# Dense GELU forward and backward on one core: x's first block without overlap, w1 in four parts, the first pair's halves side by side

## The chip, the cores and the metric

The kernel runs on one core of a Trainium2 chip. The time is device microseconds (us) of one execution, as the median of several runs; lower is better. A profiled execution gives the trace from which the views below come.

## The reference

`x` is [2048, 448], `w1` [448, 1792], `w2` [1792, 448], all bf16. Computed are the forward output and the gradients of all five inputs for a given `grad_out`:

```python
h = gelu_tanh(x @ w1 + b1)
out = h @ w2 + b2
# and, by jax.vjp with grad_out: grads of x, w1, b1, w2, b2
```

## The kernel before

The 2048 rows of x are four blocks of 512 columns once turned (xT), and the 1792 hidden units are 14 tiles of 128, taken two at a time: 28 pairs, pair p in block p // 7. All work is laid down in four lists, one for each engine, that set the order of its instructions: PE_ORDER for TensorE (PE), ACT_ORDER for ScalarE (ACT), DVE_ORDER for VectorE (DVE) and SP_ORDER for the queue that issues most DMAs. An engine runs its list from left to right and waits where an item's inputs or its place are not ready; nothing overtakes.

The names in the lists, with a pair's number p:

- On PE, `W` are wake matmuls of constants and `X` the transposes of x's first block. `u` is x times w1 for a pair (`h` is the same for one half of pair 0's columns), `q` is grad_out times w2 turned, `p` and `o` are h times w2 (the output), and `x1.` and so on are the gradient of x. `B` spreads b2 over all partitions.
- `c` copies a pair's `u` out of its two banks and adds b1 (A is the first tile, B the second; on ACT or DVE). `s` (square), `g` (GELU) and `t` (tanh) are ACT's, `e r y z m n` are DVE's; together they make h and the derivative's factors. `G` multiplies them with `q`, which stands in the banks qb.
- `vo` and `vx` copy output and x's gradient from their banks, `So` and `Sx` store them, `H` and `T` store h and turn the gradient of h.
- Loads: `xr` followed by two tile numbers is rows of x, `L` a part of w1's first 384 rows, `R` w1's last rows, `K` a part of w2, `X` and `Y` on SP are x and grad_out turned by the DMA, `J` and `I` are w2 and w1 turned, `E` small ends.

448 is three and a half tiles of 128. So `u` and `q` are done as matmuls of half height, 64 rows, in slots of two side by side: one in the upper half of the array for one tile of the pair, one in the lower half for the other (`uq_run`). A pair has a run `.1` and a run `.2`, between which the halves change banks; before a run that writes banks which the other half wrote last, PE waits for a word from POOL that the earlier run has ended (`run`). For this the fourth tile of xT holds the last 64 columns of x in its upper half and in its lower half the first 64 once more, shifted by one row, which the overlapping load of 512 columns gives (each row of 448 and 64 of the next). w1's fourth tile holds its last 64 rows (R0, R1) and its first 64 (R2, R3).

The first pair is an exception: its two halves of 256 columns, h0.0 and h1.0, are done by `full_run` with 16 matmuls, 12 over 128 rows and 4 over 64. After x's transposes come, in order, B, the first pair, u1 to u3 and then p0.0, the first output piece. `u` uses banks 4 and 5, but pairs 1 and 2 use 0 and 1, 2 and 3 (`U_BANK`); p's items use 0 to 3.

The u copies stand in buffers ub that pairs share by the table `UB`. When all 28 pairs are done, PE runs the two gradients of w1 (L755) and w2 (L809).

Of the kernel before, what the change touches and what calls it, by code (L numbers as in the profile page):

```python
# [96 lines left out]
x0.1.0.6.1 q9.1 u16.1 q9.2 u16.2 x0.0.0.6.2 q10.1 u17.1 q10.2 u17.2 x0.1.0.6.2 q11.1 x0.0.6.10.1 u18.1 q11.2 u18.2
x0.1.6.10.1 x0.0.6.10.2 x0.1.6.10.2 u19.1 q12.1 u19.2 q12.2 x0.0.10.14.1 u20.1 x0.1.10.14.1 u20.2 x0.0.10.14.2
x0.1.10.14.2 q13.1 o2.0.0.6.1 q13.2 o2.1.0.6.1 o2.0.0.6.2 o2.1.0.6.2 q14.1 o2.0.6.10.1 q14.2 o2.1.6.10.1 o2.0.6.10.2
q15.1 u21.1 q15.2 u21.2 o2.1.6.10.2 o2.0.10.14.1 o2.1.10.14.1 u22.1 q16.1 u22.2 q16.2 o2.0.10.14.2 u23.1 o2.1.10.14.2  # L100
u23.2 q17.1 x1.0.0.6.1 x1.1.0.6.1 q17.2 x1.0.0.6.2 x1.1.0.6.2 x1.0.6.10.1 x1.1.6.10.1 q18.1 x1.0.6.10.2 u24.1 q18.2
u24.2 x1.1.6.10.2 x1.0.10.14.1 x1.1.10.14.1 q19.1 x1.0.10.14.2 q19.2 u25.1 x1.1.10.14.2 u25.2 q20.1 x2.0.0.6.1 q20.2
x2.1.0.6.1 u26.1 x2.0.0.6.2 u26.2 x2.1.0.6.2 q21.1 x2.0.6.10.1 u27.1 q21.2 u27.2 x2.1.6.10.1 x2.0.6.10.2 x2.1.6.10.2
q22.1 x2.0.10.14.1 q22.2 x2.1.10.14.1 x2.0.10.14.2 x2.1.10.14.2 q23.1 o3.0.0.6.1 q23.2 o3.1.0.6.1 o3.0.0.6.2
o3.1.0.6.2 q24.1 o3.0.6.10.1 q24.2 o3.1.6.10.1 o3.0.6.10.2 o3.1.6.10.2 q25.1 o3.0.10.14.1 q25.2 o3.1.10.14.1
o3.0.10.14.2 q26.1 o3.1.10.14.2 q26.2 x3.0.0.6.1 x3.1.0.6.1 q27.1 x3.0.0.6.2 q27.2 x3.1.0.6.2 x3.0.6.10.1 x3.1.6.10.1
# [52 lines left out]
def make_plan(tc, ctx, x, w1, b1, w2, b2, grad_out, out_0, out_1, out_2, out_3, out_4, out_5):  # L159
# [113 lines left out]
    def full_run(w, t, banks, pair, c0, c1):  # L275

        two = []
        for i in (0, 1):
            ft = 2 * (pair % NPB) + i
            for k in range(4):  # L280
                rows = slice(0, 128) if k < 3 else slice(0, 64)
                two.append((k == 3, i, k, lambda i=i, k=k, ft=ft, rows=rows: nc.tensor.matmul(  # L282
                    bk_(banks[i])[:, 0:c1 - c0], lhsT=w[rows, k, ft * P:(ft + 1) * P], rhs=t[rows, k, EDGE + c0:EDGE + c1],
                    start=(k == 0), stop=(k == 3), skip_group_check=True)))
        for _, _, _, product in sorted(two, key=lambda m: m[:3]):
            product()

# [24 lines left out]
    def U(p, d, hf=None):  # L312
# [7 lines left out]
        rd = [part_w1(p), ("w1r", int(p % NPB > 3))] + [("xT", b, h) for h in hs]  # L320
# [3 lines left out]
        if d == 2:  # L324
            rd += [("xe", b), ("w1f", int(p % NPB > 3))]
# [73 lines left out]
    def C(p, h, eng, hf=None):  # L399
# [8 lines left out]
        if eng == "ACT":  # L408
            fn = lambda: nc.scalar.activation(out=out, in_=src, func=ACT.Identity, bias=bias)  # L409
        else:  # L410
            fn = lambda: nc.vector.tensor_scalar(out=out, in0=src, scalar1=bias, scalar2=None, op0=ALU.add)  # L411
# [441 lines left out]
```

## Time and profile before

| | |
|---|---|
| median of 3 runs | 266.15 us (266.08 to 266.22) |
| profiled execution | 265.99 us, span 264.2 us |
| TensorE clock granted | 1.00 |
| PE busy | 260.4 us (99%) |
| DVE busy | 198.9 us (75%) |
| ACT busy | 130.6 us (49%) |
| DMA | 46.10 MB, mean 175 GB/s |

The profiled execution lies 0.16 us under the median, and 1.8 us of it are outside the span. Busy time is a share of the whole span; the first 13 us, in which loads, transposes and the first pairs follow on one another, have other limits than the rest. PEld is PE's loading of weights, which runs beside its matmuls. L238 in a row is the line in `run` through which nearly all matmuls of half height go.

### The profile page before, as it was taken

What the parts mean: (1) busy time and instruction counts of PE and PEld (TensorE: products, weight loads), DVE (VectorE), ACT (ScalarE), POOL (GpSimd) and SP (SyncE); (2) the same over time, 40 slices, a digit from 0 to 9 for tenths busy, and PEclk for the clock granted to TensorE, in tenths of its full rate; (3) what the DMA queues carried; (4) which work ended last, traced back from release to release, by engine and by line L of the source; (5) the groups of instructions that cost most, each with busy time, mean ns of one, the idle gap of its engine ahead of it and who ended that gap; (6) DMA issues with size and microseconds to landing.
All of it is one profiled execution on the core that took longest, in us unless ns stands there. A gap on an engine that the chain in (4) does not pass through costs nothing.

```text
span 264.2 us, 5339 instructions
## 1 busy us (share of the span) xinstructions
PE 260.4 (99%) x2170; PEld 182.7 (69%) x2170; DVE 198.9 (75%) x289; ACT 130.6 (49%) x168; POOL 14.1 (5%) x8
## 2 busy tenths in 40 slices
PE   8999999999999999999999999999999999999995
PEld 4488988888888886677777777765555555555554
DVE  6887998999998789897876998339999999311000
ACT  4899786996998936736696511011112111000001
POOL 0000000000000000000000000000000393400000
PEclk9999999999999999999999999999999999999999
DMA  7999689999999953393665934794799988984221
GB/s 199 278 189 257 118 174 189 333 243 257 229 219 197 231 139 66 87 223 85 74 173 160 291 99 104 132 309 108 164 228 158 168 218 171 244 157 130 69 72 35
DMA packets 120235, 46.10 MB, mean 175 GB/s; under 512 B 96671, under 2 KB 120081, under 8 KB 120210
## 3 DMA queue, kind: packets, MB, share of 16 engines
q1 hardware_dynamic: 119636, 45.43, 76.6%
q8 instruction: 17, 0.28, 0.4%
q10 hardware_dynamic: 574, 0.33, 0.4%
q14 instruction: 8, 0.07, 0.1%
HBM read 7.70 MB, written 14.28 MB: 83 GB/s over the span
## 4 chain that ended last, share of the span: by engine, by line
PE 97%; ACT 1%; DVE 1%; issue 0%; ACTq 0%; DVEq 0%
PE bank L238 46%; PE bank L755 16%; PE bank L809 16%; PE qb L238 16%; PE qb L365 1%; ACT TR L427 1%; PE bank L282 1%; PE bank L564 1%; DVE ub L411 0%; ACT ub L409 0%; DVE TR L432 0%; DVE TR L437 0%; PE qb L630 0%; ACT w_sb L814 0%; ACTq L427 0%
## 5 line engine op out<-in xcount | busy, mean ns | idle before, releaser
L238 PEld LDWEIGHTS <-HG 64*128 64x128 bf16 x896 | 70.9, 94 | 17.8 <-issue 0.7
L238 PE MATMUL qb<-gT,w2Tf 64*128 64x512 bf16 x392 | 55.9, 376 | 0.0
L238 PE MATMUL bank<-xT,w1f 64*128 64x512 bf16 x378 | 53.4, 376 | 0.0
L238 PE MATMUL bank<-w_sb,HG 64*128 64x448 bf16 x448 | 51.2, 349 | 0.4 <-ACT ub L409 0.4
L238 PE MATMUL bank<-w1T_sb,HG 64*128 64x448 bf16 x448 | 48.4, 349 | 0.0
L809 PE MATMUL bank<-w2Tf,HG 128*128 128x448 bf16 (+2 forms) x240 | 42.6, 340 | 0.0
L755 PE MATMUL bank<-w1f,gh_nat 128*128 128x448 bf16 x224 | 42.5, 352 | 0.0
L467 DVE SCALAR_TENSOR_TENSOR HG<-TR,qb 128x1024 bf16<-128x1024 bf16 x28 | 34.1, 1217 | 9.6 <-PE qb L238 9.4
L238 PEld LDWEIGHTS <-w2Tf 64*128 64x128 bf16 x392 | 32.6, 94 | 8.2 <-issue 0.2
L238 PEld LDWEIGHTS <-w1f 64*128 64x128 bf16 x378 | 31.4, 94 | 8.3 <-issue 0.3
L809 PEld LDWEIGHTS <-HG 128*128 128x128 bf16 x240 | 22.9, 98 | 19.8
L755 PEld LDWEIGHTS <-gh_nat 128*128 128x128 bf16 x224 | 21.8, 98 | 20.6 <-issue 0.4
L452 ACT ACTIVATE TR<-TR 128x1024 bf16<-128x1024 bf16 x28 | 29.3, 1050 | 11.3 <-DVE TR L442 11.3
L778 DVE TENSOR_TENSOR w1T_sb<-w1T_sb,gh_nat 128x1792 f32<-128x1792 f32 x14 | 28.4, 2025 | 0.5
L457 DVE TENSOR_SCALAR TR<-TR 128x2048 bf16<-128x2048 bf16 x28 | 19.3, 689 | 8.3 <-ACT TR L452 8.3
L760 ACT ACTIVATE TR<-bank 128x448 bf16<-128x448 f32 x14 | 7.6, 543 | 34.9 <-PE bank L755 34.9
L815 DVE CAST w_sb<-bank 128x448 bf16<-128x448 f32 x6 | 3.7, 624 | 25.9 <-PE bank L809 25.9
L814 ACT CAST w_sb<-bank 128x448 bf16<-128x448 f32 (+2 forms) x9 | 4.4, 490 | 37.7 <-PE bank L809 37.7
L784 POOL PARTITION_ALL_REDUCE w1T_sb<-w1T_sb x1 | 10.7, 10662 | 208.3 <-DVE w1T_sb L782 208.3
L409 ACT ACTIVATE ub<-bank,b1T 128x512 bf16<-128x512 f32 (+1 forms) x26 | 16.2, 666 | 10.9 <-DVE TR L442 6.0
L462 DVE TENSOR_TENSOR TR<-TR 128x1024 bf16<-128x1024 bf16 x28 | 19.2, 686 | 0.2
L447 DVE TENSOR_TENSOR TR<-TR,HG 128x1024 bf16<-128x1024 bf16 x28 | 19.2, 684 | 0.0
(45 smaller groups left out, 183.6 us busy)
## 6 DMA issues: line engine op xcount, KB each, us to landing
hT_dram<-HG SPq DMA_DIRECT2D x28, 256.0 KB, 3.4
out_dram<-st SPq DMA_DIRECT2D x16, 224.0 KB, 2.7
w1f<-in_x_dram SPq DMA_DIRECT2D x2, 896.0 KB
w2Tf<-in_grad_out_dram SPq DMA_DIRECT2D x2, 560.0 KB
out_dram<-w_sb SPq DMA_DIRECT2D x2, 448.0 KB, 2.7
out_dram<-xT SPq DMA_DIRECT2D x2, 384.0 KB, 3.1
w_sb<-in_w_dram SPq DMA_DIRECT2D x1, 672.0 KB
w2Tf<-in_grad_out_dram SPq DMA_DIRECT2D x1, 672.0 KB, 4.6
```

What stands on the lines that cost most here:

```text
L238: m = nc.tensor.matmul(bk_(b)[:, 0:n], lhsT=l, rhs=r, start=st, stop=sp, skip_group_check=True)
L409: fn = lambda: nc.scalar.activation(out=out, in_=src, func=ACT.Identity, bias=bias)
L447: pl.op("DVE", f"R{p}", lambda: nc.vector.tensor_tensor(out=t[:, 1], in0=t[:, 1], in1=hblk(p), op=ALU.mult), [("r", p), ("h", p)], [val((" ...
L452: pl.op("ACT", f"t{p}", lambda: nc.scalar.activation(out=t[:, 0], in_=t[:, 0], func=ACT.Tanh), [("y", p)], [val(("t", p), ("TR0", p % NTR) ...
L457: pl.op("DVE", f"m{p}", lambda: nc.vector.tensor_scalar(out=t[:], in0=t[:], scalar1=1.0, scalar2=None, op0=ALU.subtract), [("t", p), ("r2" ...
L462: pl.op("DVE", f"n{p}", lambda: nc.vector.tensor_tensor(out=t[:, 0], in0=t[:, 0], in1=t[:, 1], op=ALU.mult), [("m0", p), ("m1", p)], [val( ...
L467: pl.op("DVE", f"G{p}", lambda: nc.vector.scalar_tensor_tensor(out=ghblk(p), in0=t[:, 0], scalar=2.0, in1=qb[:, :, :], op0=ALU.subtract, o ...
L755: nc.tensor.matmul(bk_(bk)[:, 0:D], lhsT=gh_nat[:, st // 4, ft, st % 4, :], rhs=x_nat[:, st, :], start=(st == 0), stop=(st == NS - 1))
L760: fn = (lambda dst=dst, src=src: nc.scalar.mul(out=dst, in_=src, mul=-0.5)) if eng == "ACT" else \
L778: nc.vector.tensor_tensor(out=hs3, in0=a, in1=gh_nat[:, st // 4, :, st % 4, :], op=ALU.add)
L784: pl.op("POOL", "gb1", lambda: nc.gpsimd.partition_all_reduce(gb1_w, hsum, channels=P, reduce_op=bass_isa.ReduceOp.add), ["hsc"], ["gb1"], ...
L809: nc.tensor.matmul(bk_(bk)[:, 0:d1 - d0], lhsT=h_nat[ft][:, st, :], rhs=g_nat[:, st, d0:d1], start=(st == 0), stop=(st == NS - 1))
```

## The change

Loads. x's first block is read as it is, 448 columns a row, and the fourth tile of xT gets x's last 128 columns (320 to 447). For it a new tile w1z holds w1's last 128 rows; it lies in a stretch of gh_nat that is not yet used then, and comes in three parts (Z0, Z1 on ACT, Z2 on SP). L now has four parts of 256, 512, 512 and 512 columns in place of five. R and F are the last and the first 64 rows of w1 in one load each, first needed by block 1. b1 and b2 are issued by SP, tiles 0 and 1 of x change queues, and K3 is ahead of K2.

Products. In block 0 `u` goes through `plain`: run .1 has four slots and run .2 three, both from unshifted rows, and the edge copy Dx0 is gone. The first pair does the same in its two halves (h0.1, h0.2, h1.1, h1.2); `full_run` is gone. B runs over 64 rows, of which all but one are zero, and stands between h0.1 and h0.2. Pair 3 uses the banks of qb, and u4.1 stands ahead of p0.0.

The four lists are new throughout: W6 for W7, q0.1 behind more p's, output pieces split at 5 and 10 tiles in place of 6 and 10, many B copies on DVE, 14 ub buffers in place of 10 for the first half.

```diff
-W7 X0 X1 X2 X3 B h0.0 h1.0 u1.1 u2.1 u1.2 u3.1 u2.2 u3.2 p0.0 p0.1 u4.1 p0.2 p0.3 u4.2 p1.0 p1.1 p1.2 u5.1 p1.3 p2.0
+W6 X0 X1 X2 X3 h0.1 B h0.2 h1.1 u1.1 h1.2 u1.2 u2.1 u3.1 u2.2 u3.2 u4.1 p0.0 u4.2 p0.1 p0.2 p0.3 u5.1 p1.0 u5.2 p1.1
...
-xr01 L0 b1 b2 table X1 X3 c0A0 c0A1 s0 g0 c1A s1 c2A c3A s2 g1 g2 c4A g3 g4 t0 c5A t1 g5 s3 s4 c6A t2 g6 c7A s5 g7 t3
+xr12 L0 Z0 Z1 table X1 X3 c0A0 c0A1 s0 g0 s1 c2B c3A s2 c4A g1 g2 g3 c5A g4 g5 t0 c6A t1 g6 s3 s4 c7A t2 g7 c8A s5 g8
...
-ident X0 X2 Dx0 b1T c0B0 c0B1 b2c e0 r0 c1B z0 y0 c2B c3B e1 r1 y1 e2 z1 r2 c4B z2 y2 Dg0 c5B m0 n0 m1 n1 c6B G0 m2 e3 n2
+ident X0 b1T X2 b2c c0B0 c0B1 c1A c1B e0 r0 y0 c2A z0 e1 c3B c4B r1 e2 y1 r2 z1 c5B z2 y2 c6B m0 n0 m1 n1 c7B m2 Dg0
+n2 c8B G0 e3 r3 c9B z3 y3 G1 vo0.2 m3 vo0.3 vo0.0 vo0.1 n3 G2 e4 c11B r4 e5 z4 r5 y4 z5 G3 m4 e6 n4 r6 y5 z6 y6 c13B
...
-xr12 xr24 R0 L1 R2 L2 L3 R1 K0 L4 K1 R3 K2 Y0 X1 J0 K3 J1 J2 E J3 I0 I1 Y1 X2 So0.1 H0 H1 H2 H3 H4 H5 H6 H7 H8 T0 T1
+xr01 xr24 b1 b2 L1 L2 Z2 K0 K1 F L3 R K3 K2 X1 J0 Y0 J1 I0 J2 Y1 E J3 I1 So0.1 X2 So0.0 H0 H1 H2 H3 H4 H5 H6 H7 H8 H9
...
-U_BANK = {1: 0, 2: 2}
+U_BANK = {1: 0, 2: 2, 3: 6}
+ACT_FIRST = (3,)
...
+    w1z = gh_nat[:, 1, :, :, :].rearrange("p f s c -> p (f s c)")[:, 0:F]
...
+        def plain(i, k, low, st, sp):
+            rows = slice(0, 64) if low else slice(64, 128)
+            cols = slice(ft[i] * P, (ft[i] + 1) * P)
+            return (banks[i], c1 - c0, w[rows, k, cols] if k < 3 else w1z[rows, cols], t[rows, k, EDGE + c0:EDGE + c1], st, sp)
+
+        if w is w1_sb and pair < NPB:
+            if d == 1:
+                run([(plain(1, k, True, k == 0, False), plain(0, k, False, k == 0, False)) for k in (0, 1, 2, 3)])
+            else:
+                run([(plain(0, k, True, False, k == 2), plain(1, (0, 1, 3)[k], False, False, k == 2)) for k in (0, 1, 2)])
+            return
...
-    W1_PART = (0, 1, 2, 3, 4, 4, 4)
-    W1_COLS = ((0, 256), (256, 512), (512, 768), (768, 1024), (1024, 1792))
+    W1_PART = (0, 1, 1, 2, 2, 3, 3)
+    W1_COLS = ((0, 256), (256, 768), (768, 1280), (1280, F))
+    REST = (0, 1, 1, 2, 2, 2, 2)
+    REST_COLS = ((0, 256), (256, 768), (768, F))
...
-        if d == 0:
-            pe(f"u{p}.{d}{tag}", lambda: full_run(w1_sb, xT[b % 2], bk, p, *c), rd, vs, ("s256", 8), (None, 0))
-            return
...
-        src = bass.AP(tensor=x2.tensor, offset=x2.offset + t0 * P * D, ap=[[D, P], [P * D, t1 - t0], [1, 4 * P]])
+        src = x2[t0 * P:t1 * P, :].rearrange("(t p) d -> p t d", p=P)
...
+                c = min(k * P, D - P)
-                nc.tensor.matmul(bk_(t)[:, k * P:(k + 1) * P], lhsT=x_rows[:, t, k * P:(k + 1) * P], rhs=ident,
+                nc.tensor.matmul(bk_(t)[:, k * P:(k + 1) * P], lhsT=x_rows[:, t, c:c + P], rhs=ident,
...
-            pe("b2u", lambda: nc.tensor.matmul(bk_(6)[:, 0:D], lhsT=one[0:1, 0:P], rhs=stage[NST - 1][0:1, 0, :], start=True, stop=True,
+            pe("b2u", lambda: nc.tensor.matmul(bk_(6)[:, 0:D], lhsT=one[0:64, 0:P], rhs=stage[NST - 1][0:64, 0, :], start=True, stop=True,
```

How the instructions stand on PE in the first pair. Before, in the middle of h0.0 and at the start of h1.0 (xT0 is x's first block turned, w1f holds w1; bank4 and bank5 are the first half's banks, bank2 and bank3 the second's):

```order
L282 MATMUL bank5_94<-xT0_68,w1f_64 128x256
L282 LDWEIGHTS w1f_64 [waits DMAHW5_49]
L282 MATMUL bank4_93<-xT0_68,w1f_64 128x256
L282 LDWEIGHTS w1f_64
L282 MATMUL bank5_94<-xT0_68,w1f_64 128x256
L282 LDWEIGHTS w1f_64 [waits DVE_49]
L282 MATMUL bank2_91<-xT0_68,w1f_64 128x256 [waits Activation_49]
```

Now, at the end of h0.1, B and the start of h0.2 (gh_nat holds w1z, st2 holds b2):

```order
L240 LDWEIGHTS gh_nat_74 [waits DMAHW4_49]
L240 MATMUL bank5_94<-xT0_68,gh_nat_74 128x256
L240 LDWEIGHTS gh_nat_74
L240 MATMUL bank4_93<-xT0_68,gh_nat_74 128x256
L651 LDWEIGHTS const-bfloat16-1.0
L651 MATMUL qb_88<-st2_83,const-bfloat16-1.0 128x448 [waits DMAHW7_49]
L240 LDWEIGHTS w1f_64 [waits Pool_sequencer_49]
L240 MATMUL bank4_93<-xT0_68,w1f_64 128x256
```

The w1 tail now comes from w1z and waits for Z0, B has moved from ahead of the pair into it, and the run behind B waits for POOL.

How they stand on ACT from the first pair's copies to the copy of u4. Before (TR and HG are the targets of s and g, ub and gh_nat of the copies):

```order
L409 ACTIVATE ub0_75<-bank2_91,b1T_86 128x256 [waits PE_49]
L427 ACTIVATE TR0_78<-ub0_75 128x1024 [waits DVE_49,Activation_49]
L422 ACTIVATE HG_73<-ub0_75 128x1024
L409 ACTIVATE ub1_76<-bank0_89,b1T_86 128x512 [waits PE_49]
L427 ACTIVATE TR1_79<-ub1_76 128x1024 [waits DVE_49,Activation_49]
L409 ACTIVATE ub2_77<-bank2_91,b1T_86 128x512 [waits PE_49]
L409 ACTIVATE gh_nat_74<-bank4_93,b1T_86 128x512 [waits PE_49]
L427 ACTIVATE TR2_80<-ub2_77 128x1024 [waits DMAHW3_49,DVE_49,Activation_49]
```

And now:

```order
L410 ACTIVATE ub0_75<-bank2_91,b1T_86 128x256 [waits DVE_49,PE_49]
L435 ACTIVATE TR0_78<-ub0_75 128x1024 [waits DVE_49,Activation_49]
L430 ACTIVATE HG_73<-ub0_75 128x1024
L435 ACTIVATE TR1_79<-ub1_76 128x1024 [waits DVE_49]
L410 ACTIVATE ub2_77<-bank3_92,b1T_86 128x512 [waits PE_49]
L410 ACTIVATE gh_nat_74<-qb_88,b1T_86 128x512 [waits PE_49]
L435 ACTIVATE TR2_80<-ub2_77 128x1024 [waits DMAHW3_49,DVE_49,Activation_49]
L410 ACTIVATE gh_nat_74<-bank4_93,b1T_86 128x512 [waits PE_49]
```

c1A has left ACT for DVE, c2B stands in place of c2A, pair 3 is copied from qb, and c4A has moved ahead of g1 and g2.

How SP's first loads stand. Before (TR2 takes x's rows, w2_sb w2):

```order
L507 DMA TR2_80<-in_x_dram 128x512
L507 DMA TR2_80<-in_x_dram 128x2x512
L507 DMA w1f_64<-in_w1_dram 64x1024
L507 DMA w1f_64<-in_w1_dram 128x3x256
L507 DMA w1f_64<-in_w1_dram 64x1024 [waits DMAHW0_49]
L507 DMA w1f_64<-in_w1_dram 128x3x256 [waits DMAHW1_49]
```

And now:

```order
L516 DMA TR2_80<-in_x_dram 128x448
L516 DMA TR2_80<-in_x_dram 128x2x448
L516 DMA b1n_85<-in_b1_dram 14x128 [waits Pool_49]
L516 DMA st2_83<-in_b2_dram 1x448 [waits Pool_49]
L516 DMA w1f_64<-in_w1_dram 128x3x512 [waits DMAHW0_49]
L516 DMA w1f_64<-in_w1_dram 128x3x512 [waits DMAHW1_49]
L516 DMA gh_nat_74<-in_w1_dram 128x1024 [waits DMAHW2_49]
```

There are eight DMA semaphores, used in turn; the ninth load and each behind it waits until the load that had its semaphore has landed. L1 was the second load of w1 on SP and waited for nothing; now b1 and b2 are ahead of it, and it waits for xr12.

More of the change, by code (lines that the diff above doesn't have):

```diff
@@ L97 @@
[L97 to L106, printed above, removed]
@@ L273, in unit_run @@
         run(slots)
[L275 to L286, printed above, removed]
     def gap(bank):
@@ L319, in U @@
             vs = [bank(("u", p, 0, hf), bk[0]), bank(("u", p, 1, hf), bk[1])]
[L320 to L325 removed]
+        rd = [part_w1(p)] + [("xT", b, h) for h in hs] + ([("w1z", REST[p])] if b == 0 else ["w1r"])
+        if d == 2 and b > 0:
+            rd += [("xe", b), "w1f"]
         pe(f"u{p}.{d}{tag}", lambda: uq_run(w1_sb, xT[b % 2], bk, p, d, *c), rd, vs,
@@ L411, in C, with after @@
             fn = lambda: nc.vector.tensor_scalar(out=out, in0=src, scalar1=bias, scalar2=None, op0=ALU.add)
-        pl.op(eng, f"c{p}{'AB'[h]}{'' if hf is None else hf}", fn, [uv, "b1T"], [v], ("copy", 512 if hf is None else 256))
+        o = pl.op(eng, f"c{p}{'AB'[h]}{'' if hf is None else hf}", fn, [uv, "b1T"], [v], ("copy", 512 if hf is None else 256))
+        if hf is None and u_banks(p)[0] == 6 and f"c{p}B" in DVE_ORDER.split() and f"c{p}A" in ACT_ORDER.split():
+            if eng == ("DVE" if p in ACT_FIRST else "ACT"):
+                after(o, [("u", p, 1 - h)])
+    def after(o, vs):
+        o["after"] = vs
+        return o
     def hblk(p):
@@ L712, in make_plan @@
         elif t == "Nx":
-            rows_nat("xn", x_nat, x2, [("w1", i) for i in range(len(W1_COLS))] + [("w1r", 0), ("w1r", 1), ("w1f", 0), ("w1f", 1)])
+            rows_nat("xn", x_nat, x2, [("w1", i) for i in range(len(W1_COLS))] + ["w1r", "w1f"])
         elif t == "Ng":
```

97 lines of the change are left out of this document (56 added, 41 removed).

## The prediction

> **What bounds the kernel now.** I read the page first: the engines' busy shares and the chain that ended last.
>
> ```profile
> PE 260.4 (99%) x2170; PEld 182.7 (69%) x2170; DVE 198.9 (75%) x289; ACT 130.6 (49%) x168; POOL 14.1 (5%) x8
> PE 97%; ACT 1%; DVE 1%; issue 0%; ACTq 0%; DVEq 0%
> ```
>
> TensorE (PE) is busy 99% of the span and makes up 97% of the chain, so a change pays only where it removes PE slots or stretches in which PE waits. Then the chain in order of time, for those stretches.
>
> ```profile
> 8.58 1.06 ACT TR L427
> 10.56 0.67 DVE ub L411
> 11.31 1.06 ACT TR L427
> 12.99 10.13 PE bank L238 x98
> 23.77 0.76 PE bank L238 x8
> 24.52 0.86 PE qb L238 x8
> ...
> 176.64 42.48 PE bank L755 x224
> 219.12 42.43 PE bank L809 x240
> ```
>
> Between 8.58 and 12.99 the chain leaves PE for ACT and DVE; behind that it is PE alone. Two matmuls of half height make a slot, so 8 are four slots: 0.86 / 4 = 0.216 us at 512 columns, 0.76 / 4 = 0.189 us at 448. From u1.1 to 176.64 the list holds 385 slots of the first kind (27 u and 28 q of 7) and 448 of the second: 83.3 + 84.7 = 167.95 us. PE's own timeline shows where this stretch begins.
>
> ```profile
> 3.27 0.63 PE L365 MATMUL qb<-const-bfloat16-1.0 128*128 128x512 bf16 x1
> ...
> 5.37 0.36 PE L630 MATMUL qb<-st,const-bfloat16-1.0 1*128 1x448 bf16 x1
> 5.66 2.12 PE L282 MATMUL bank<-xT,w1f 128*128 128x256 bf16 x15
> 7.51 0.39 PE L238 MATMUL bank<-xT,w1f 64*128 64x512 bf16 x1
> ...
> 12.99 1.05 PE L238 MATMUL bank<-w_sb,HG 64*128 64x448 bf16 x8 [0.39 <-ACT ub L409]
> ```
>
> u1.1 starts at 7.51, and 7.51 + 167.95 = 175.46 against 176.64: 1.18 us are lost. The 21 slots from u1.1 to p0.0 would end at 12.05, and p0.0 starts at 12.99, so 0.94 of the 1.18 lie there and only 0.24 in the 163 us behind. (The 0.39 in brackets is smaller because the modelled ends cover the rest.) A gap shows in the weight loads, too:
>
> ```profile
> 8.54 3.57 PEld L238 LDWEIGHTS <-w1f 64*128 64x128 bf16 x35 [0.28 <-issue]
> ```
>
> The first gap, at 8.54, is u2.1 waiting for banks 2 and 3, which the first pair's second half held. In the second, ahead of 12.99, p0.0 waits for the same banks until ACT has copied u2. ACT's and DVE's timelines tell why that is late.
>
> ```profile
> 7.82 0.47 ACT L409 ACTIVATE ub<-bank,b1T 128x256 bf16<-128x256 f32 x1 [0.26 <-PE bank L282]
> ...
> 9.54 1.04 ACT L422 ACTIVATE HG<-ub 128x1024 bf16<-128x1024 bf16 x1
> 10.49 0.67 ACT L409 ACTIVATE ub<-bank,b1T 128x512 bf16<-128x512 f32 x1
> 11.31 1.06 ACT L427 ACTIVATE TR<-ub 128x1024 bf16<-128x1024 bf16 x1 [0.15 <-DVE ub L411]
> 12.28 0.67 ACT L409 ACTIVATE ub<-bank,b1T 128x512 bf16<-128x512 f32 x1
> 12.85 0.68 ACT L409 ACTIVATE gh_nat<-bank,b1T 128x512 bf16<-128x512 f32 x1
> ```
>
> The copy at 12.28 is c2A, queued behind c1A and s1. Back to back, ACT starts the next instruction 0.95 us after one of 1024 columns and 0.57 after a copy.
>
> **The first pair, side by side.** Before, from 5.37 to 7.51: B, then 16 matmuls of 256 columns, with a change between full and half height at each regrouping; 2.14 us. Now 28 half matmuls in 14 slots of 256 / 512 x 0.216 = 0.108, without such changes: 1.52 us, of which h1.2 (0.33) stands behind u1.1. h0.1 needs the copy of X1, done at 5.39 before and, with x's rows an eighth shorter, an estimated 0.1 us earlier. So h0.1 starts at 5.36 and ends at 5.80, B at 5.99. h0.2 swaps the halves' banks right behind B, so it waits for POOL's word that h0.1 has ended; no run before stands that close. Bounds: 0, since B may cover it, and 0.2, the longest such wait among PE's weight loads.
>
> ```profile
> PEld L238 <- POOLq L233: 0.3, 2, 0.2
> ```
>
> I take 0.1: h0.2 ends at 6.42. h1.1 needs the copy of X2, now behind b1T on DVE: 4.28 + 0.69 (X0) + 0.85 (b1T) + 0.69 = 6.5, by these rows:
>
> ```profile
> 4.37 0.69 DVE L571 CAST xT<-bank 128x512 bf16<-128x512 f32 x1 [0.78 <-PE bank L564]
> ...
> 6.13 0.85 DVE L648 STREAM_TRANSPOSE b1T<-b1n 32x32 bf16<-32x32 bf16 x4
> ```
>
> So h1.1 runs from 6.53 to 6.97, u1.1 starts there, 0.54 earlier, and owes 0.33 for h1.2: 0.21 gained. The edge copy (Dx0, one column on DVE) goes at no price, since DVE had idle time there; POOL's one more memset lies in the 2 us before x arrives.
>
> **Loads.** SP issues L1 only when the landing of xr12 has freed a DMA semaphore; before, the load in that place (R2) waited for x in the same way and went out at 3.69:
>
> ```profile
> 1.17 0.42 SPq L507 DMA_DIRECT2D TR<-in_x_dram  x1
> ...
> 3.69 0.48 SPq L507 DMA_DIRECT2D w1f<-in_w_dram  x1
> ...
> 9.30 5.68 SPq L519 DMA_TRANSPOSE gT<-in_grad_out_dram  x1
> ```
>
> So L1 goes out near 3.6. It is twice as large as before (393 KB), and u1.1 and u2.1 both need it. The rates at which loads moved, and how long some took:
>
> ```profile
> 2.00:4.50 2.50, 2.50 (x13) 1.21 (x11) 1.50 (x9) 1.49 (x2) 0.00 (x0) 1.00 1.00 318
> 4.50:7.00 2.50, 2.50 (x23) 1.62 (x21) 2.21 (x7) 1.17 (x2) 0.00 (x0) 1.00 1.03 235
> ```
>
> ```profile
> TR<-in_x_dram SPq DMA_DIRECT2D x1, 256.0 KB, 3.4
> w1f<-in_w_dram SPq DMA_DIRECT2D x1, 576.0 KB, 6.3
> gT<-in_grad_out_dram SPq DMA_TRANSPOSE x1, 9.2
> ```
>
> Ahead of L1 are 857 KB (x 459, L0 197, Z0 66, Z1 131, the biases 4): 795 KB by 4.5 at 318 GB/s, the rest by 4.75. L1 then takes 1.24 us at the rate of x's 1024-byte runs (318), or 1.67 at that of the 512-byte runs that followed (235). Its own runs are 1024 bytes, so I take 1.24. To that comes the time from the last byte to the landing, estimated from xr24: issued at 1.17, it landed 3.4 later, at 4.57, while the 0.72 MB up to its end were moved near 4.1. With 0.5, L1 lands at 6.5, inside 6.97. From the x and w1f rows, by size between 262 KB (3.4) and 590 KB (6.3), 393 KB would take 4.6 us and land at 8.2: a wait of 1.2 us as upper bound. The later parts of w1 and w2 land in the order of their use. The first transposed load, Y0, was issued at 9.30 and landed 9.2 later, at 18.5; now X1 is the first, with 0.85 MB more in front of it (w1z and K3, less x's overlap), 2.7 to 3.6 us at the two rates: 21.2 to 22.1. u7.1, the first to read it, stands at 22.4 by the slots.
>
> **The gap at p0.0.** u1.1, h1.2 and u1.2 run to 8.82. A copy starts some 0.2 behind its last slot, so c0A1 and c0B1 (0.47) end at 8.85, and u2.1, which needs their banks, waits 0.08. c1A and c1B are both DVE's (9.0 to 10.4), s1 runs straight behind g0 at 10.8, c2B at 11.75 to 12.45, c2A on DVE to 12.45. u4.1 uses banks 4 and 5, free since h0, because u3 has moved to the qb banks; with it in front, p0.0 comes up at 8.90 + 18 slots = 12.80 and finds everything ready. The 0.94 shrinks to 0.08. Late next is c5A: behind c4A (14.03, when u4.2 has ended) stand g1, g2, g3, so it ends at 14.03 + 0.57 + 3 x 0.95 + 0.67 = 18.12, and u6.1, due at 17.99, waits 0.18.
>
> **DVE.** It takes the B copies of pairs 8, 9, 11, 13, 14 and others from ACT, some 0.67 us each (the chain's 10.56 row). It had little room from 40 to 60, 19.02 of 20 us busy:
>
> ```profile
> 40.00:60.00 20.00, 20.00 (x200) 17.90 (x197) 19.02 (x32) 17.60 (x22) 0.00 (x0) 1.00 1.08 258
> ```
>
> ```profile
> 37.80 2.22 DVE L487 TENSOR_TENSOR st<-bank,b_bc 128x448 bf16<-128x448 f32 x4
> 39.93 1.21 DVE L467 SCALAR_TENSOR_TENSOR HG<-TR,qb 128x1024 bf16<-128x1024 bf16 x1
> 41.06 0.69 DVE L442 TENSOR_TENSOR TR<-TR,gh_nat 128x1024 bf16<-128x1024 bf16 x1
> 41.66 0.68 DVE L462 TENSOR_TENSOR TR<-TR 128x1024 bf16<-128x1024 bf16 x1
> ```
>
> Steps here are 1.13 for G, 0.55 for vo, 0.60 for the rest. The new list starts q0 some 6 us later, which gives room; the tightest place is q3.1, due at 40.3, which needs G2. G1 starts at 34.3 when q1.2 has ended; then 1.13 + 4 x 0.55 + 2 x 0.60 = 4.53, so G2 runs 38.85 to 40.06: 0.2 to spare. I cost DVE at nothing; with that cover gone, each 0.1 of DVE costs PE 0.1.
>
> **Sum.** 6.97 + 0.33 + 167.95 + 0.08 + 0.18 + 0.24 (as before) = 175.75 in place of 176.64, 0.9 us earlier; the last two stages keep their lists. The profiled execution took 265.99 (span 264.20), so 265.1; the median of the runs shown is 0.16 higher, and the forecast **265.3 us**. About 0.2% (0.53 us) is what a measurement here can tell from no change.
>
> **Rivals.**
>
> *The clock stays at half longer (slower).* W6 is one wake matmul less: the seventh started at 3.27, so the sixth ends there, and x's transposes cannot start before 3.6, a gap of 0.35 us that W7 just filled.
>
> ```profile
> L564 PEld LDWEIGHTS <-TR x14: 104/151/152, 3.7 to 5.0; 128*128 128x128 bf16 x14
> L564 PEld LDWEIGHTS <-TR x3: 98/108/151, 5.0 to 5.2; 128*128 128x128 bf16 x3
> ```
>
> PE came up to speed at about 5.1 us (weight loads 151 ns before, 98 after), 4.3 us after the first wake matmul. If the gap costs it the same stretch of some 3 us again, the 3.1 us from h0.1 to about 8.5, less 0.2 of waits, run at half speed: 1.45 us lost, 266.75 in all, and from 1.43 lost the kernel is slower by over 0.2%. It decides whether x's second transposes still run at 151 ns behind 5.2; for: nothing in this trace starts PE with a hole; against: the hole is a tenth of the stretch. The Trainium skill, "TensorE: Matmul & The Clock Gate", section "Part 1: The HAM clock gate", says the full clock comes after one busy window of about 3.4 us in a free-running count. By that rule the window that closed at 5.1 holds the gap, and the next closes at 8.5; how much idleness it forgives the page does not say. 0.09.
>
> *L1 is late (slower).* Price one for one behind 6.97. The gain is gone at 7.9, and from 8.4 the kernel is slower by over 0.2%, with L1 at 8.7 267.0. For: the upper bound of 8.2; against: the 576 KB row had K0 in front of it. 0.08.
>
> *The wait moves to DVE and ACT.* The margins of 0.2 at q3.1 and of -0.18 at u6.1 are as small as the rows are rough; DVE's 1.0 us of idle time between 40 and 60 stands against four more copies between 28 and 60 (2.7). If PE waits 0.7 more, 266.0: no change. 0.20.
>
> *x's second block is late.* Y0 took 5.7 us to issue in a full queue, and X1 meets a fuller one; with X1 at 24 u7.1 waits 1.6, 266.9. It decides at 22.4; for: the margin is only 0.3 at the slower rate; against: larger runs moved faster. 0.06.
>
> **How the numbers follow.** The forecast has 0.57: nearly all of it faster. Rival by rival, DVE/ACT gives 0.03 faster, 0.14 same, 0.03 slower; clock 0.02 and 0.07, L1 0.03 and 0.05, X1 0.01 and 0.05 (same and slower); 0.02 of the forecast falls within. Faster 0.58, same 0.22, slower 0.20. With every wait at zero (0.08 + 0.18 + 0.1) the time is 264.9; a little under that and the rivals up to 266.9 make the range, 264.8 to 266.9.
>
> **What would show it.** Right: h0.1 near 5.4, u1.1 near 7.0, no gap at p0.0, q0.1 near 28.4, the last L238 slot ending near 175.8. Wrong: weight loads of 151 ns behind 5.2; a DMA wait at u1.1 or u7.1; DVE busy without a hole while PE waits at a q; a last slot at or behind 176.6.

## The result and the profile after

| | before | after |
|---|---|---|
| median | 266.15 us (265.94 to 266.81, 20 runs) | 265.74 us (265.52 to 266.22, 20 runs) |
| profiled execution, span | 265.99, 264.2 | 265.63, 263.9 |
| ratio, 95% interval | | 0.9983 (0.9976 to 0.9990) |

By the medians the change makes the kernel 0.41 us (0.15%) faster, about half of the 0.85 forecast.

The page after, busy times and then the chain by engine:

```profile
PE 259.9 (98%) x2181; PEld 187.4 (71%) x2181; DVE 205.4 (78%) x300; ACT 124.1 (47%) x156; POOL 14.5 (5%) x9
PE 97%; DVE 1%; issue 0%; ACT 0%
```

PE still carries the chain. ACT has left it (it was 1%); DVE's 1% now lies ahead of the first transpose. The chain in order of time, at the last two stages:

```profile
176.31 42.48 PE bank L775 x224
218.79 42.43 PE bank L829 x240
```

Both stages start 0.33 earlier than before (176.64 and 219.12) and last as long: all of the gain arises ahead of them. In before's timeline the first transpose stands here, for comparison:

```profile
3.74 1.70 PE L564 MATMUL bank<-st,TR 128*128 128x128 bf16 x16
```

The timeline of after, from the start to p0.0:

```profile
0.86 0.47 POOL L665 MEMSET st<- 64x448 bf16 x1
0.89 1.22 DVE L561 TENSOR_SCALAR st<-st 128x1 bf16<-128x1 bf16 x5
...
3.41 0.93 SPq L516 DMA_DIRECT2D w1f<-in_w_dram  x2
...
3.99 1.80 PE L574 MATMUL bank<-st,TR 128*128 128x128 bf16 x16 [0.51 <-DVE st L567]
...
5.72 0.50 PE L240 MATMUL bank<-xT,w1f 64*128 64x256 bf16 x6
...
6.17 0.35 PE L651 MATMUL qb<-st,const-bfloat16-1.0 64*128 64x448 bf16 x1
...
6.44 0.22 PEld L240 LDWEIGHTS <-w1f 64*128 64x128 bf16 x5 [0.29 <-POOLq L235]
...
6.96 0.22 PEld L240 LDWEIGHTS <-w1f 64*128 64x128 bf16 x6 [0.29 <-DVE xT L581]
...
7.55 0.33 PEld L240 LDWEIGHTS <-w1f 64*128 64x128 bf16 x6 [0.26 <-DMA w1f<-in_w_dram]
...
9.06 1.95 DVE L412 TENSOR_SCALAR ub<-bank,b1T 128x256 bf16<-128x256 f32 x3 [1.23 <-PE bank L240]
...
9.59 0.33 PEld L240 LDWEIGHTS <-w1f 64*128 64x128 bf16 x5 [0.32 <-issue]
...
13.47 0.56 PE L240 MATMUL bank<-w_sb,HG 64*128 64x448 bf16 x4
```

The gap at p0.0 is gone: its row at 13.47 has no bracket, where before had one. But u1.1 starts at 7.55, as late as before (7.51), and h1.2 still stands behind it. Three waits lie ahead of it: the transposes wait for DVE's identity until 3.99 (before 3.74), h1.1 for X2's copy until 6.96, u1.1 for L1. The windows of after, DMA's rate in the last column:

```profile
2.00:4.50 2.50, 1.99 (x10) 0.84 (x9) 1.59 (x9) 1.49 (x2) 0.00 (x0) 1.00 1.00 305
4.50:5.50 1.00, 1.00 (x12) 1.00 (x11) 0.86 (x2) 0.46 (x1) 0.00 (x0) 1.00 0.65 124
4.50:7.00 2.50, 2.49 (x30) 1.74 (x30) 2.29 (x7) 1.19 (x3) 0.00 (x0) 1.00 0.84 236
5.50:7.50 2.00, 1.99 (x27) 1.00 (x24) 1.93 (x7) 1.18 (x3) 0.00 (x0) 1.00 0.99 322
...
40.00:60.00 20.00, 20.00 (x202) 18.28 (x200) 19.73 (x34) 13.81 (x16) 0.00 (x0) 1.00 0.97 259
```

From 4.5 to 5.5 the DMA engines moved 124 GB/s in place of 305: most of the loads ahead had been moved, and L1, issued at 3.41, had hardly begun. And DVE is full from 40 to 60 (19.73 of 20) while PE has no hole.

By this trace: 7.55 + 0.33 (h1.2) + 167.95 (slots) + 0.19 (u2.1) + 0.29 (the rest) = 176.31, where the chain has L775. Before, 1.18 us were lost behind u1.1; now it is 0.48, which is 0.70 won. The start of the kernel gives 0.37 of that back: u1.1 is 0.04 later, and h1.2's 0.33 comes on top.

### The profile page after: what moved, and what is told of

Same layout as the page of the kernel before. It is cut to its first block, busy times and chain, and to the rows that moved or that the text cites. A ratio compares the mean times of both kernels' runs of the same rounds, so it can differ in the third digit from the quotient of the medians.

```text
span 263.9 us, 5349 instructions
## 1 busy us (share of the span) xinstructions
PE 259.9 (98%) x2181; PEld 187.4 (71%) x2181; DVE 205.4 (78%) x300; ACT 124.1 (47%) x156; POOL 14.5 (5%) x9
## 4 chain that ended last, share of the span: by engine, by line
PE 97%; DVE 1%; issue 0%; ACT 0%
PE bank L240 48%; PE qb L240 17%; PE bank L775 16%; PE bank L829 16%; PE bank L574 1%; DVE st L561 0%; DVE st L564 0%; DVE st L567 0%; ACT w_sb L834 0%; PE qb L651 0%; DVE st L558 0%
## 5 line engine op out<-in xcount | busy, mean ns | idle before, releaser
L240 PEld LDWEIGHTS <-HG 64*128 64x128 bf16 x896 | 73.9, 94 | 14.6 <-POOLq L235 1.7
L240 PE MATMUL qb<-gT,w2Tf 64*128 64x512 bf16 x392 | 57.8, 376 | 0.0
L240 PE MATMUL bank<-xT,w1f 64*128 64x512 bf16 (+1 forms) x371 | 53.3, 370 | 0.0
L240 PE MATMUL bank<-w_sb,HG 64*128 64x448 bf16 x448 | 51.8, 349 | 0.0
L240 PE MATMUL bank<-w1T_sb,HG 64*128 64x448 bf16 x448 | 51.0, 349 | 0.0
L775 PE MATMUL bank<-w1f,gh_nat 128*128 128x448 bf16 x224 | 42.5, 353 | 0.0
L240 PEld LDWEIGHTS <-w2Tf 64*128 64x128 bf16 x392 | 35.3, 94 | 6.0 <-POOLq L235 0.5
L775 PEld LDWEIGHTS <-gh_nat 128*128 128x128 bf16 x224 | 21.8, 98 | 20.6 <-issue 0.4
L435 ACT ACTIVATE TR<-gh_nat 128x1024 bf16<-128x1024 bf16 x15 | 15.5, 1051 | 10.9 <-DVE TR L470 10.9
```

Source lines behind the costliest of these rows:

```text
L240: m = nc.tensor.matmul(bk_(b)[:, 0:n], lhsT=l, rhs=r, start=st, stop=sp, skip_group_check=True)
L435: pl.op("ACT", f"s{p}", lambda: nc.scalar.activation(out=TR[p % NTR][:, 1], in_=ubuf(p), func=ACT.Square, scale=sc), [("ub", p)], [v], ("a ...
L775: nc.tensor.matmul(bk_(bk)[:, 0:D], lhsT=gh_nat[:, st // 4, ft, st % 4, :], rhs=x_nat[:, st, :], start=(st == 0), stop=(st == NS - 1))
```

## Experiments

My theory: the gap at p0.0 brought the gain, and two delays at u1.1 that hide each other, the late identity and the late L1, took half of it back. Rivals: only one of the two counts; what is won at the start is waited for again later; the clock. All twelve kernels, times in us; before was measured again beside them, with medians of 266.20 to 266.25, so the ratios compare kernels better than the medians do. The last two columns come from the one profiled execution's timeline, in which the first matmul of L755 or L775 starts 0.07 ahead of the chain's time for it:

| kernel | median (lowest to highest) | ratio to before, 95% interval | u1.1 starts | L755/L775 starts |
|---|---|---|---|---|
| before | 266.15 (265.94 to 266.81) | | 7.51 | 176.57 |
| after | 265.74 (265.52 to 266.22) | 0.9983 (0.9976 to 0.9990) | 7.55 | 176.24 |
| one_row | 265.67 (265.48 to 266.43) | 0.9978 (0.9964 to 0.9992) | 7.53 | 176.22 |
| one_z | 265.55 (265.51 to 265.70) | 0.9974 (0.9964 to 0.9984) | 7.51 | 176.19 |
| one_row_one_z | 265.55 (265.28 to 267.55) | 0.9984 (0.9970 to 0.9998) | 7.44 | 176.12 |
| memset_twice | 265.72 (265.53 to 267.39) | 0.9988 (0.9977 to 0.9999) | 7.58 | 176.26 |
| p00_first | 266.61 (266.40 to 266.99) | 1.0008 (0.9993 to 1.0023) | 7.43 | 176.99 |
| before_c2a | 266.47 (266.16 to 266.93) | 1.0003 (0.9989 to 1.0018) | 7.70 | 177.12 |
| one_row_l1 | 265.86 (265.60 to 269.65) | 0.9996 (0.9979 to 1.0012) | 7.66 | 176.35 |
| one_row_l1_x2 | 266.05 (265.67 to 268.48) | 1.0012 (0.9992 to 1.0032) | 7.79 | 176.48 |
| before_u4 | 267.02 (266.68 to 267.59) | 1.0021 (1.0008 to 1.0035) | 7.75 | 177.66 |
| l1_half | 266.04 (265.19 to 266.99) | 0.9980 (0.9964 to 0.9996) | 6.75 | 176.10 |
| w7 | 265.79 (265.47 to 266.32) | 0.9970 (0.9946 to 0.9994) | 7.73 | 176.42 |
| l1_half_k2 | 265.73 (265.25 to 267.19) | 0.9983 (0.9970 to 0.9996) | 7.61 | 176.29 |

Most intervals reach about 0.3 us or more to each side, so differences of 0.1 to 0.3 between these kernels cannot be read from the medians. Nor can small ones be read from one trace each: p00_first has the same instructions as after up to u3.2, and yet u1.1 starts at 7.43 there and at 7.55 in after; before_c2a and before, alike up to c1A, have 7.70 and 7.51. A trace does show which wait held a row. In the edits below, lines are cut to the part that changes, and lines that only follow from those shown are left out.

### The memset beside the identity: one_row, memset_twice

```diff
-lhsT=one[0:64, 0:P], rhs=stage[NST - 1][0:64, 0, :]
+lhsT=one[0:1, 0:P], rhs=stage[NST - 1][0:1, 0, :]
-    pl.op("POOL", "b2z", lambda: nc.gpsimd.memset(stage[NST - 1][0:64, 0, :], 0.0), [], ["b2z"], ("tiny", 1))
```

> The changed kernel with B over one row again, so that POOL's memset of b2's 64 rows is gone. Theory: that memset, running beside DVE's five small identity steps, stretched them (1.22 us against 0.98) and so held x's transposes back to 3.99; without it the five steps take about 1.0, the first transpose starts near 3.7, h0.1 near 5.45. But u1.1 is held at 7.55 by the landing of L1 (7.50), so the time stays that of the changed kernel, 265.7 (0.4 under before), within 0.1. Rival A, the late transposes alone hold u1.1: 265.4, u1.1 near 7.25. Rival B, the memset has nothing to do with the identity: five steps still 1.2 us, time 265.7.

In memset_twice the line stays and its memset is done two times.

> The changed kernel with POOL's memset of b2's rows done twice (0.94 us instead of 0.47). Theory: the identity steps that run beside it are stretched further, by another 0.1 to 0.25, the transposes start at 4.1 to 4.25, PE is then later than L1 and the time rises by 0.1 to 0.25, to 265.8 to 265.95. Rival, the memset does not touch DVE: five steps 1.22 as in the changed kernel, transposes at 3.99, time 265.7 (b2 then leaves 0.47 later, which nobody waits for).

The timeline of one_row, and below it that of memset_twice (DVE L668 makes b1T, which stands ahead of X2's copy in DVE's list):

```profile
0.89 0.98 DVE L560 TENSOR_SCALAR st<-st 128x1 bf16<-128x1 bf16 x5
...
1.08 0.17 DVE L560 TENSOR_SCALAR st<-st 128x2 bf16<-128x2 bf16 x1
...
5.30 0.85 DVE L668 STREAM_TRANSPOSE b1T<-b1n 32x32 bf16<-32x32 bf16 x4 [0.46 <-DMA b1n<-in_b_dram]
...
6.92 0.22 PEld L240 LDWEIGHTS <-w1f 64*128 64x128 bf16 x6 [0.44 <-DVE xT L580]
...
7.53 0.33 PEld L240 LDWEIGHTS <-w1f 64*128 64x128 bf16 x6 [0.27 <-DMA w1f<-in_w_dram]
```

```profile
0.86 0.99 POOL L665 MEMSET st<- 64x448 bf16 x2
0.89 1.40 DVE L561 TENSOR_SCALAR st<-st 128x1 bf16<-128x1 bf16 x5
...
4.16 1.78 PE L574 MATMUL bank<-st,TR 128*128 128x128 bf16 x16 [0.68 <-DVE st L567]
```

No memset, one, two: the five steps take 0.98, 1.22, 1.40, and the transposes start at 3.73, 3.99, 4.16. That the memset stretches the identity is shown. At the end it costs nothing that these runs can tell: without it u1.1 still waits for L1 and starts 0.02 earlier; doubled, 0.03 later, and the three ratios have intervals that overlap. But L1 is not alone in that. Without the memset h1.1 itself starts only 0.04 earlier (6.92 for 6.96), because b1T waits 0.46 for b1's load and X2's copy stands behind it on DVE: a third delay, which my theory lacked. The lower end that I gave for memset_twice (0.1) was too high, since in after PE still came ahead of L1 at u1.1.

### L1 issued earlier: one_z, one_row_one_z, one_row_l1, one_row_l1_x2

```diff
-xr12 L0 Z0 Z1 table
+xr12 L0 Z0 table
...
-    REST_COLS = ((0, 256), (256, 768), (768, F))
+    REST_COLS = ((0, 768), (768, F))
```

> The changed kernel with Z0 and Z1 as one load, so that one load fewer stands ahead of L1 and it need not wait for a semaphore. Theory: L1 is issued near 2.4 instead of 3.41 and lands near 6.5 instead of 7.50; PE, which had come up at 7.52 in the changed kernel, gains only 0.03, and the time stays 265.7, within 0.1. Rival, L1 alone holds the start: u1.1 near 7.2, 265.4.

> Both edits together: B over one row and no memset, Z0 and Z1 as one load. Theory (the two delays hide each other): only here does u1.1 move, to about 7.2 to 7.25 behind h1.1, which waits for the copy of X2 (ending near 6.6); the time falls by 0.3 to 265.4. Rival: one of the two alone is the cause, and this kernel is as fast as the better of the two singles. Second rival: what is won at the start is waited for again at u2.1 or at a q, and the time stays 265.7.

The timelines of one_z and of one_row_one_z:

```profile
2.44 1.43 SPq L516 DMA_DIRECT2D w1f<-in_w_dram  x2
...
6.33 0.10 PEld L240 LDWEIGHTS <-gh_nat 64*128 64x128 bf16 x2 [0.36 <-DMA gh_nat<-in_w_dram]
```

```profile
6.16 0.10 PEld L240 LDWEIGHTS <-gh_nat 64*128 64x128 bf16 x2 [0.62 <-DMA gh_nat<-in_w_dram]
```

L1 no longer holds u1.1, but h0.1 now waits for w1z, whose load had grown from 66 to 197 KB; that it also met L1's packets is not shown. So one_z does not show what the late identity costs by itself. Of the 0.3 expected together, 0.11 came in the traces, no more than p00_first and after differ without any cause. By the medians one_row_one_z is as fast as one_z alone (265.55 both), so the first rival (only one of the two counts) is not excluded. The second (the win waited for later) has no support: the 0.11 is still there at the last stages. I then left Z0 and Z1 as they were, kept one_row's edit and moved L1 ahead of b2 (the last two lines below) and, in the second kernel, X2 ahead of b1T too:

```diff
-ident X0 b1T X2 b2c
+ident X0 X2 b1T b2c
...
-xr01 xr24 b1 b2 L1 L2 Z2
+xr01 xr24 b1 L1 b2 L2 Z2
```

> B over one row without the memset, the loads of w1z as in the changed kernel, and L1 issued ahead of b2, so that L1 has an unused semaphore. Theory: the merged Z0 had landed too late (6.1 to 6.3) in the two kernels that had it; here Z0 lands near 5.2 as in the changed kernel, L1 is issued near 2.2 and lands near 6.3, and h1.1 waits only for the copy of X2 behind b1T (6.9). u1.1 near 7.35, time 265.5. Rival: b2, now behind L1, lands after 6.0 and B holds PE instead; u1.1 stays at 7.5 and the time 265.65.

> As the kernel before it, and X2's copy ahead of b1T in DVE's list. Theory: h1.1 no longer waits for X2; u1.1 near 6.85, 0.7 earlier than in the changed kernel, the time 265.1, the best of all. Rival A: b1T, now later, holds the first pair's copies and u2.1 waits for what was won: 265.5. Rival B: the transposed load of x, which landed at 22.18 in the changed kernel, becomes the bound of u7.1 (22.63 there, 21.9 here) and gives half back: 265.3.

The chain of one_row_l1, its row of the windows, and the timeline of one_row_l1_x2:

```profile
2.17 5.45 DMA w1f<-in_w_dram
```

```profile
4.50:5.50 1.00, 0.77 (x16) 0.65 (x13) 0.95 (x3) 0.89 (x2) 0.00 (x0) 1.00 0.86 270
```

```profile
6.74 0.34 PE L650 MATMUL qb<-st,const-bfloat16-1.0 1*128 1x448 bf16 x1 [0.62 <-DMA st<-in_b_dram]
```

Both missed. In one_row_l1, L1, issued 1.24 earlier than in after, landed at 7.62, no earlier than the 7.55 at which u1.1 began there, although 270 GB/s now flowed from 4.5 to 5.5, where after had 124. In one_row_l1_x2, b2, now behind L1, held B until 6.74. The issue time alone was not the lever, and by this profile neither was the hole in the flow.

### Fewer bytes ahead: l1_half, l1_half_k2

Besides one_row's edit and X2 ahead of b1T:

```diff
-b1 b2 L1 L2 Z2 K0 K1 F L3 R
+b1 b2 L1 L2 L3 Z2 K0 K1 F L4 R
...
-    W1_COLS = ((0, 256), (256, 768), (768, 1280), (1280, F))
+    W1_COLS = ((0, 256), (256, 512), (512, 768), (768, 1280), (1280, F))
```

> The changed kernel with L1 in two parts of 256 columns again (197 KB each instead of 393), B over one row without the memset, and X2's copy ahead of b1T. Theory: what holds u1.1 is how many bytes stand ahead of its last load, not when that load is issued; with 197 KB less in front, the first half lands near 6.9 and u1.1 starts at 6.9 to 7.0, 0.55 to 0.6 earlier than in the changed kernel: 265.1 to 265.2, below both kernels. Rival: the loads share the 16 engines, so that the half lands little earlier than the whole (7.3 or later), or b2 or Z0 holds PE instead as in the two kernels with an early L1: 265.5 to 265.7.

The timeline of l1_half:

```profile
6.75 0.33 PEld L240 LDWEIGHTS <-w1f 64*128 64x128 bf16 x6 [0.16 <-DMA w1f<-in_w_dram]
...
19.55 0.56 PE L240 MATMUL bank<-w_sb,HG 64*128 64x448 bf16 x4 [0.48 <-DMA w_sb<-in_w_dram]
```

L1 is still the last that u1.1 waits for, but with half the bytes it lets it go at 6.75, 0.80 earlier; 197 KB at 236 GB/s, the rate of after from 4.5 to 7.0, would be 0.83. The halving needs the other two edits beside it: with X2's copy behind b1T, as in one_row, h1.1 starts only at 6.92 and u1.1 could not come before about 7.35. No run has X2 ahead of b1T with L1 whole and loaded as in after, so the shares of the edits are not separated. The 0.80 lasts until p2.0, which waits for K2 and starts no earlier than in after (19.55 and 19.52); at the last stages 0.14 of it is left, and the forecast of 265.1 to 265.2 missed (266.04). So K2 went ahead of K3 again.

```diff
-L4 R K3 K2 X1
+L4 R K2 K3 X1
```

> As the kernel with L1 in two parts, and K2 (w2's tiles 4 to 7, 459 KB) issued ahead of K3 (tiles 8 to 13, 688 KB) as in the kernel before. There u1.1 began at 6.75 and PE was 0.80 ahead of the changed kernel up to p2.0, which then waited for K2's landing at 19.51 and lost 0.66 of it. Theory: with K3 behind it K2 lands 2 us earlier, p2.0 waits for nothing, and the next transfer that PE meets, x's second block (landed at 22.22, needed by u7.1 near 22.2), takes little: the matmul ahead of the last two stages starts 0.6 to 0.8 earlier than in the changed kernel, time 265.0 to 265.1. Rival: K3, now last, is late at p4.0 (24.1), or x's block at u7.1, and half or more is lost again: 265.4 or more.

PE's weight loads of w1 in l1_half_k2 up to 8.2 (least, median and most ns, first and last start), and its timeline:

```profile
L240 PEld LDWEIGHTS <-w1f x23: 92/95/149, 5.5 to 7.8; 64*128 64x128 bf16 x23
```

```profile
5.53 0.82 PE L240 MATMUL bank<-xT,w1f 64*128 64x256 bf16 x6
```

p2.0 no longer waited. But in this execution the clock came up only behind 6 us: six matmuls of h0.1 take 0.82 where l1_half has 0.50, some weight loads 149 ns, and u1.1 starts at 7.61. The two kernels stand alike on PE, ACT and DVE, and on SP up to R, behind w1's last part; and between the first transpose and u1.1 l1_half_k2 shows no wait for a DMA, so that the slow clock is what sets these 0.86 apart. Whether l1_half_k2 is faster than after therefore stays open; by its median (265.73 against 265.74) it isn't, and the 265.0 to 265.1 expected did not come.

### The gap at p0.0: p00_first, before_c2a, before_u4

```diff
-u3.2 u4.1 p0.0 u4.2
+u3.2 p0.0 u4.1 u4.2
```

> The changed kernel with p0.0 ahead of u4.1 again (one swap in PE's list). Theory: the gap at p0.0 is worth what the chain of before showed; p0.0 comes up at 12.6, its banks are u2's, whose copies end at 13.06 (DVE) and 13.16 (ACT), so PE waits 0.55 to 0.6 there and never gets it back: 266.2 to 266.3, about the time of before. Rival: the wait is given back later (u4.2 or u6.1 finds its copies sooner), and the time stays 265.7.

```diff
-c0A0 c0A1 s0 g0 c1A s1 c2A c3A s2
+c0A0 c0A1 s0 g0 c1A c2A s1 c3A s2
```

> The kernel before with c2A ahead of s1 in ACT's list, nothing else. Theory: the copy that ended the gap at p0.0 then runs at 11.3 instead of 12.28, p0.0 starts at 12.3 to 12.5 instead of 12.99, and the time falls by about 0.5 to 265.65, as much as the whole change brought. Rival: s1 and with it DVE's steps of pair 1 come 0.6 later, and PE waits at p1.0 or later for what it won: 266.15.

```diff
-U_BANK = {1: 0, 2: 2}
+U_BANK = {1: 0, 2: 2, 3: 6}
-u3.2 p0.0 p0.1 u4.1
+u3.2 u4.1 p0.0 p0.1
```

> The kernel before with one part of the change alone: pair 3 uses the banks of qb and u4.1 stands ahead of p0.0 and p0.1; loads, first pair and all other lists as before. Theory: this part alone fills the gap at p0.0. Both of u2's copies ended near 13 in before (moving one of them alone gained nothing), so p0.0 starts near 13.1 still, but three slots of u4.1 (0.65) now stand ahead of it: 0.5 to 0.6 less, 265.6, as fast as the whole change or faster. Rival: u3's copies out of qb, or u4's that come later on, make PE wait for it within the next pairs, and the time stays 266.2.

The timelines of p00_first, of before_c2a, of before (the copy c2B) and of before_u4, in this order:

```profile
7.43 0.33 PEld L240 LDWEIGHTS <-w1f 64*128 64x128 bf16 x6
...
13.00 0.63 PE L240 MATMUL bank<-w_sb,HG 64*128 64x448 bf16 x4 [0.33 <-DVE ub L412]
...
14.59 0.33 PEld L240 LDWEIGHTS <-w1f 64*128 64x128 bf16 x5 [0.60 <-POOLq L235]
```

```profile
11.94 0.69 ACT L409 ACTIVATE ub<-bank,b1T 128x512 bf16<-128x512 f32 x1 [0.60 <-PE bank L238]
...
12.52 0.75 DVE L411 TENSOR_SCALAR ub<-bank,b1T 128x512 bf16<-128x512 f32 x1
...
13.32 0.91 PE L238 MATMUL bank<-w_sb,HG 64*128 64x448 bf16 x7 [0.30 <-DVE ub L411]
```

```profile
12.34 0.74 DVE L411 TENSOR_SCALAR ub<-bank,b1T 128x512 bf16<-128x512 f32 x1
```

```profile
13.44 0.33 PEld L238 LDWEIGHTS <-w1f 64*128 64x128 bf16 x6 [1.11 <-DMA w1f<-in_w_dram]
...
18.36 0.82 PE L238 MATMUL bank<-xT,w1f 64*128 64x512 bf16 x6 [0.41 <-DVE gh_nat L411]
```

p00_first shows that u4.1's place carries the gain: one swap makes the last stages start 0.75 later and the median 0.87 higher (0.67 by the ratios, 1.0008 and 0.9983, whose intervals do not meet), back at before's or behind it. It is a little more than expected, because p0.0 also stood between u4.1 and u4.2; side by side, u4.2 waits 0.60 for POOL's word. In this profile u1.1 does not wait for L1: its row at 7.43 has no bracket.

before_c2a refutes my reading of before's chain. ACT's c2A moved forward by 0.34, ending at 12.63, but DVE's c2B (12.52 to 13.27) was just as late, and from its second slot p0.0 waits for that. In before, too, c2B ended at 13.08 (12.34 + 0.74), right behind c2A's 12.95; the chain named c2A, because p0.0's first slot needs its bank. Moving one of two late copies brings nothing. (Here b2 also landed late, so that u1.1 starts 0.19 later than in before: part of the 0.55 by which the last stages, at 177.12 for 176.57, are late.)

before_u4 says why the loads belong to the change: u4.1 reads w1's columns from 1024, in before's cut the fifth part, and waits for it until 13.44. In after, with columns 768 to 1280 in one part that is loaded earlier, u4.1 starts at 12.61 without a wait and fills the gap; other cuts were not run. This part of the change alone is a loss of 0.77 by the medians (0.56 by the ratio); in its profile the last stages start 1.09 late, of which u1.1, at 7.75 for 7.51, has 0.24.

### The clock: w7

```diff
-W6 X0 X1 X2 X3
+W7 X0 X1 X2 X3
```

> The changed kernel with seven wake matmuls instead of six. Theory: the seventh ends near 3.7, ahead of the first transpose at 3.99, and so costs nothing; the clock may come up at 5.1 instead of 5.6, which makes some of the transposes faster, but u1.1 waits for L1: time 265.7, within 0.1. Rival, the cold transposes (all 16 weight loads at 147 ns) are what delays u1.1: 265.4.

PE's weight loads for the transposes in w7, and its timeline:

```profile
L574 PEld LDWEIGHTS <-TR x16: 98/147/147, 4.0 to 5.4; 128*128 128x128 bf16 x16
```

```profile
7.73 0.33 PEld L240 LDWEIGHTS <-w1f 64*128 64x128 bf16 x6 [0.45 <-DMA w1f<-in_w_dram]
```

Almost all transposes are slow with W7 too; u1.1 waits for L1, and the median is 0.05 above after's (ratios 0.9970 and 0.9983, with intervals that overlap). That the sixth wake matmul is the last, and the hole behind it, cost nothing that these runs can tell; one profile for each cannot say how often the clock is late with W6 and with W7.

## Why the prediction was right, and where it missed

The direction, the place of the gain and the range (264.8 to 266.9) held; the size was twice too large. Step by step:

- **u1.1's start, the step that failed.** Forecast 6.97, measured 7.55, so 0.58 of the sum's error; with 0.11 more at u2.1, 0.05 more in the rest and 0.18 less at u6.1, that is the 0.56 between 175.75 and 176.31. Most of the 0.58 is PE's own lateness and not L1's: h1.1 starts at 6.96 where the forecast has 6.53, so with its 0.44 PE could have begun u1.1 at about 7.40, and in p00_first, where nothing waits for L1, it does at 7.43. L1 adds the last 0.12 to 0.15. Two prices of the sections on the first pair and on the loads were wrong.
  - "POOL's one more memset lies in the 2 us before x arrives" was priced at nothing; it held DVE's identity, and with it the first transpose, by 0.25. h1.1 needs X2's copy, which DVE makes behind the identity, X0 and b1T, and comes 0.43 late. Without the memset (one_row) it was not earlier by 0.25 but by 0.04, since b1T then waited for b1's load, which the forecast took as being there. Of the other 0.18, about 0.1 had been taken off for x's shorter rows, which X0's copy does not show (it starts 0.62 behind the first transpose, before 0.63); the rest is some 0.03 between each step on DVE and the next.
  - L1's landing was forecast at 6.5, from 318 GB/s without a break, and u1.1 was let go at 7.55. The hole of one microsecond at 124 GB/s would be worth 1 - 124/322 = 0.6 us, but that it is the cause is not shown: one_row_l1 filled it, and L1 landed no earlier. What did move the landing is fewer bytes (l1_half).
  - one_row shows that L1 hid the late identity. The reverse is not shown, since in one_z the load of w1z held h0.1.
- **The inside of the first pair** was right, though 0.36 to 0.43 late throughout: h0.1 to B 0.45 (forecast 0.44), h1.1 behind X2's copy, POOL's word at h0.2 about 0.1 beyond B.
- **u2.1** waits 0.19 (forecast 0.08): c0B1 starts at 9.06 on DVE and ends 0.47 later, 1.98 behind u1.1's start where I had 1.88.
- **The gap at p0.0** went as forecast, and it alone carries the gain. The prediction gave two reasons, the copies' new places and u4.1 in front; it is u4.1 that fills the gap (p00_first), and the reading that c2A alone made p0.0 late was wrong (before_c2a).
- **u6.1** waits for nothing (forecast 0.18), even in l1_half, where PE is 0.80 earlier up to p2.0.
- **DVE at no cost** was right: 19.73 of 20 us busy, no wait of PE at a q.
- **The rivals.** In after the clock did not stay at half until 8.5 with W6: w1's weight loads take 92 to 97 ns from 5.7 on. But it was not a fixed thing either (below). L1 was late as that rival has it, by 0.6 and not by more, of which PE's own lateness hid all but 0.12 to 0.15. In after no matmul waited for x's second block.
- **The signs.** Two of the signs of being wrong did show: weight loads of 147 ns up to 5.4, and a DMA wait at u1.1. The direction held in spite of them, because what was won behind u1.1 (0.70) is more than the start lost: 0.37 in place of the 0.21 gain that was forecast there. And it was luck that the 0.18 priced at u6.1 was not needed, which hid part of that miss.

## What to carry to other kernels

When two late things end close together, the chain names only one of them: before pricing a move, look at when the second one ends, and at what each instruction that comes forward reads, its loads too. Price a load by its bytes and by all that is in flight from its issue to its landing, and not by its place in the queue alone, and count a helper engine's small instruction against the engine that works beside it. A gain of a few tenths at the start is only worth what the next transfer lets through.
